# Value and output projection in chunks of 512 tokens in place of halves of a batch

## The chip, the cores and the metric

One core of a Trainium2 chip. The metric is device time in microseconds (us) of one execution. The engines are TensorE (PE: matrix products; PEld: its weight loads), VectorE (DVE), ScalarE (ACT), GpSimd (POOL) and SyncE (SP), which here only issues DMA transfers. The five run side by side, each through its own list in order.

## The reference

Sparse attention over 8 batches, 8 heads, 576 tokens and head size 64, then a gated projection of the 512 wide result:

```python
scores = scale * np.matmul(q, k.transpose(0, 1, 3, 2))
# heads 0-3: 0 <= i - j < 32; heads 4-7: j <= i and j % 32 == i % 32
attn = softmax(np.where(masks, scores, -1e9))
x = (attn @ v)                        # put together to [8, 576, 512]
gate_pre = sum(conv_w[k] * xp[:, k:k + S, :] for k in range(5))
gate = 1.0 / (1.0 + np.exp(-gate_pre))
val = x @ w_val                       # 512 x 512
return gate * val @ w_out             # 512 x 512
```

## The kernel before, in words

Features lie on the partitions (four blocks of 128, `ct` or `e`), tokens on the free axis. For each batch `b`:

- **Attention.** `attend_local` (three units) and `attend_strided` (two) make scores in PSUM (`s_ps`), a softmax on VectorE, ScalarE and GpSimd, a transpose of the weights (`t_ps` or VectorE), and the product with `v` (`x_ps`). ScalarE copies it into `xs[b % 2]`.
- **Splitting.** `split_x` writes x as a rounded part `xhi` (ScalarE) and a rest `xlo` (VectorE for `ct` 0 and 1, GpSimd for 2 and 3), so that three fast products `hi·hi`, `hi·lo`, `lo·hi` stand for one exact product. There is one pair of buffers for even and one for odd batches.
- **Gate.** `gate` runs the five-tap convolution along the tokens on VectorE, four instructions of 576 columns for each `e`, between two ScalarE instructions. For `e` 0 and 1 of batch 0, TensorE does it with diagonal matrices, which VectorE builds (128x640) in `ghi`. There is one gate buffer for each `e`.
- **Value.** `value` (line 450) takes each batch in two halves of 288 tokens: 8 groups (4 `e` x 2 halves) of 12 matmuls into one of three `m_ps` banks. VectorE multiplies the bank by the gate into `GV` (two buffers), ScalarE rounds it into `ghi`, and GpSimd writes the rest into `glo`.
- **Projection.** `project` (line 473) takes 128 tokens at a time: 12 matmuls of 512 columns over `ghi`, `glo` and `wo`, a ScalarE copy into `osb` and a DMA to `out`. 576 is 4.5 x 128, so an even batch leaves 64 tokens, which ScalarE copies to the front of `ghi` and `glo` for the next batch (`CARRY`).

Weights come as float64 and are made on the chip (`weight_rows`): each quarter is loaded, unpacked by ScalarE and VectorE, rounded by ScalarE, and its rest is written by GpSimd. For `w_val` the buffers `gate0` to `gate3` serve as scratch, for `w_out` two buffers `w64`.

All steps are recorded first and then issued in a written order, the string `SEQUENCE`. A token is a step's number; `f0x4` is four filler matmuls on zeros (line 162), which write a bank that nobody reads. Each engine, and SP with its DMA issues, keeps this order, and waits where an operand is not ready or a buffer is not free.

Of the kernel before, what the change touches and what calls it, by code (L numbers as in the profile page):

```python
# [18 lines left out]
DM = 512  # L19
# [7 lines left out]
CARRY = S % P  # L27
# [30 lines left out]
def tile_sparse_attention_moe(  # L58
# [68 lines left out]
    xhp = tiles(2, [P, 4, PADK + S], "xhi", F32R)  # L127
    xlp = tiles(2, [P, 4, PADK + S], "xlo", F32R)
    xhi, xlo = [t[:, :, PADK:] for t in xhp], [t[:, :, PADK:] for t in xlp]
    ghi = pool.tile([P, 4, CARRY + S], F32R, name="ghi")  # L130
    glo = pool.tile([P, 4, CARRY + S], F32R, name="glo")
    diags = ghi[:, :, :]
# [5 lines left out]
    gates = tiles(4, [P, S], "gate")  # L138
# [12 lines left out]
    w64 = tiles(2, [P, DM], "w64")  # L151
# [7 lines left out]
    idle = pool.tile([P, 512], BF16, name="idle")  # L159
    V.memset(idle, 0.0)  # L160
    plan.spare = [t[:, :] for t in m_ps.items[::-1] + x_ps.items]
    plan.filler = lambda at: T.matmul(out=at, lhsT=idle[:, :P], rhs=idle[:, :], start=True, stop=True)  # L162
# [138 lines left out]
    def attend_local(b):  # L301
# [3 lines left out]
        for u in range(3):  # L305
# [58 lines left out]
            if b in DIRECT:  # L364
                hi, lo = xhi[b % 2][:, 0:2, part], xlo[b % 2][:, 0:2, part]
# [55 lines left out]
    def gate(b):  # L421
        xs = xss[b % 2]
        for e in range(4):
            gt, group = gates[e], f"G{b}.{e}"
            if (b, e) in CONV:

                dg = diags[:, 2 * e:2 * e + 2, :].rearrange("p h (k w) -> p h k w", k=KC)
# [22 lines left out]
    def value(b):  # L450
        for e, hf in [(e, hf) for e in range(4) for hf in range(2)] if b in VORD else [(e, hf) for hf in range(2) for e in range(4)]:
            group = f"V{b}.{e}.{hf}"
            c0 = CARRY + hf * HALF
            x0 = hf * HALF
            vp = m_ps.next()[:, :HALF]
            terms = [(w, xx, ct) for ct in range(4)
                     for w, xx in ((wv[0], xhi[b % 2]), (wv[1], xhi[b % 2]), (wv[0], xlo[b % 2]))]
            pe(group, [
                mm(vp, w[:, ct, e * P:(e + 1) * P], xx[:, ct, x0:x0 + HALF], i == 0, i == 11)
                for i, (w, xx, ct) in enumerate(terms)])  # L460
            hi, lo = ghi[:, e, c0:c0 + HALF], glo[:, e, c0:c0 + HALF]
            held = (b, e, hf) in HELD

            gv = vp if held else GV.next()[:, :]
            dve(group, V.scalar_tensor_tensor, out=gv, in0=gates[e][:, x0:x0 + HALF], scalar=1.0, in1=vp,
                op0=ALU.add, op1=ALU.mult)
            act(group, A.copy, out=hi, in_=gv)
            if held:
                dve(group, V.tensor_tensor, out=lo, in0=gv, in1=hi.bitcast(F32), op=ALU.subtract)
            else:  # L470
                gps(group, G.tensor_tensor, out=lo, in0=gv, in1=hi.bitcast(F32), op=ALU.subtract)

    def project(b):

        odd = b % 2
        for m in range(4 + odd):
            group = f"P{b}.{m}"
            op = m_ps.next()[:, :]
            c0 = m * P + (0 if odd else CARRY)
            terms = [(gg, w, e) for e in range(4) for gg, w in ((ghi, wo[0]), (ghi, wo[1]), (glo, wo[0]))]  # L480
            pe(group, [
                mm(op, gg[:, e, c0:c0 + P], w[:, e, :], i == 0, i == 11)
                for i, (gg, w, e) in enumerate(terms)])
            osb = OSB.next()
            act(group, A.activation, out=osb, in_=op, func=AF.Copy, scale=0.5)
            r0 = b * S + m * P - (CARRY if odd else 0)
            plan.add("sp", group,
                     [(nc.sync.dma_start, dict(out=out[r0:r0 + P, :], in_=osb))])
# [8 lines left out]
    from_f64("make cw", cw64.rearrange("p c k w -> p (c k) w"), *[t[:, :4 * KC] for t in w64], whole=cw.rearrange("p c k -> p (c k)"))  # L497
# [24 lines left out]
NB = 1  # L522
PACKED = {4, 5, 6, 7}
VORD = {2, 3, 4, 5, 6, 7}
CONV = {(0, 0), (0, 1)}
ONPE = {(0, "L", u) for u in range(3)}
HELD = set()
DIRECT = {0}
SEQUENCE = """
72 18 0 23 44 30 38 68 1 3 5 17 73 32 22 2 74 71 70 37 75 7 4 21 50 8 9 19 175 40 11 46 6 76 10 25 81 12 20 15 78 27 45  # L530
13 39 14 79 24 41 16 f0x4 f0x1 f0x12 87 47 80 88 48 103 89 33 49 90 104 105 91 52 26 106 34 f0x6 119 92 107 42 93 176
120 108 269 95 121 29 94 272 205 36 96 51 77 122 99 43 109 123 53 98 f0x5 135 199 110 97 86 153 31 136 270 137 111 177
271 112 138 124 56 154 139 125 113 126 140 114 155 127 115 178 35 206 156 f0x4 100 200 128 101 273 141 116 102 130 142
62 129 143 117 85 284 54 118 83 131 299 144 55 179 84 132 157 82 57 158 201 58 181 147 285 276 159 160 278 63 64 275
207 286 145 65 133 287 146 134 148 59 161 288 151 300 60 180 149 162 66 314 289 152 61 301 202 165 445 183 166 277 163
290 292 444 164 291 182 447 171 302 150 184 172 67 f0x2 293 315 203 167 173 217 283 174 279 168 351 187 169 208 352 446
# [91 lines left out]
```

## Time and profile before

| | us |
|---|---|
| Runs: median of 3 (lowest, highest) | 309.85 (308.98, 310.96) |
| Profiled execution, its own time | 311.87 |
| Profiled execution, span | 309.9 |
| TensorE busy | 298.4 (96%) |
| VectorE busy | 231.7 (75%) |
| ScalarE busy | 228.8 (74%) |
| GpSimd busy | 192.7 (62%) |

The span runs from the first to the last instruction. A matmul's busy time overlaps its neighbours', since matmuls are pipelined: what one costs in a row of them is the distance between starts, not its duration. The granted clock of TensorE was 0.994 of full speed on average.

### The profile page before, as it was taken

Reading aid. Unit: us, or ns where it says so; the run is one execution under the profiler, and the core shown is the slowest. Engines: PE = TensorE matmul, PEld = TensorE weight load, DVE = VectorE, ACT = ScalarE, POOL = GpSimd, SP = SyncE. Lnnn points to the kernel's source line nnn. Section 1 sums busy time; section 2 is a strip of 40 time slices with the busy share of each in tenths; the row PEclk is TensorE's granted clock in tenths of the full one; section 3 lists DMA queues with packets and bytes.
Section 4 is the critical chain, followed back from the end, with each engine's and each line's share of the span. In section 5 each row is a group of like instructions: output and inputs, shape, how many; then the busy total and the mean of one; then the engine's idle time right before and its main releaser. Section 6 shows DMA issues by size and latency. Waiting matters only on the chain.

```text
span 309.9 us, 11212 instructions
## 1 busy us (share of the span) xinstructions
PE 298.4 (96%) x4773; PEld 261.6 (84%) x4773; DVE 231.7 (75%) x407; ACT 228.8 (74%) x501; POOL 192.7 (62%) x236
## 2 busy tenths in 40 slices
PE   8778999999999999999999999999999999999995
PEld 2448789988899889998899988998899789989983
DVE  4498779989989759867998788798955787595200
ACT  6367976998689887979999787967987848635221
POOL 8284999977876784738758696567456412562410
PEclk9799999999999999999999999999999999999999
DMA  7889678637485287344445245400134020011003
GB/s 227 298 238 278 234 254 228 220 90 218 139 241 189 72 264 249 108 131 140 142 144 193 76 158 188 141 29 2 70 88 143 36 105 34 3 68 70 0 34 135
DMA packets 20321, 43.99 MB, mean 142 GB/s; under 512 B 3056, under 2 KB 8944, under 8 KB 19696
## 3 DMA queue, kind: packets, MB, share of 16 engines
q1 hardware_dynamic: 20272, 43.28, 43.7%
q8 instruction: 37, 0.61, 0.8%
q14 instruction: 12, 0.10, 0.1%
HBM read 33.84 MB, written 9.44 MB: 140 GB/s over the span
## 4 chain that ended last, share of the span: by engine, by line
PE 89%; DMA 6%; DVE 1%; ACT 1%; issue 1%; POOL 0%; SPq 0%; POOLq 0%
PE m_ps L53 66%; PE x_ps L53 10%; PE s_ps L53 9%; PE t_ps L53 4%; DMA xs<-in_w_val_dram 2%; DMA KBL<-in_kL_dram 2%; DMA KBS<-in_kS_dram 1%; DVE KBL L173 1%; PE m_ps L162 1%; DVE ST L53 0%; ACT BDS L53 0%; POOL PB L53 0%; SPq L53 0%; ACT gate L53 0%; ACT osb L53 0%
## 5 line engine op out<-in xcount | busy, mean ns | idle before, releaser
L53 DVE SCALAR_TENSOR_TENSOR gate<-xs,cw,gate 128x576 f32<-128x576 f32 x120 | 110.9, 943 | 4.8 <-ACT gate L53 4.0
L53 PE MATMUL m_ps<-xhi,wv 128*128 128x288 f32 x512 | 103.7, 297 | 0.0
L53 POOL TENSOR_TENSOR glo<-GV,ghi 128x288 fp32r<-128x288 f32 x64 | 56.0, 881 | 55.6 <-ACT ghi L53 55.2
L53 PE MATMUL m_ps<-wo,ghi 128*128 128x512 f32 x288 | 90.1, 394 | 0.0
L53 PEld LDWEIGHTS m_ps<-xhi,wv 128*128 128x128 f32 x512 | 82.1, 188 | 0.8
L53 PE MATMUL m_ps<-xlo,wv 128*128 128x288 f32 x256 | 75.6, 295 | 0.0
L53 PEld LDWEIGHTS m_ps<-wo,ghi 128*128 128x128 f32 x288 | 53.0, 188 | 11.1 <-issue 0.2
L53 PE MATMUL m_ps<-wo,glo 128*128 128x512 f32 x144 | 56.2, 390 | 0.0
L53 DVE SCALAR_TENSOR_TENSOR GV<-gate,m_ps 128x288 f32<-128x288 f32 x64 | 28.3, 446 | 33.4 <-POOL glo L53 14.2
L53 PEld LDWEIGHTS m_ps<-xlo,wv 128*128 128x128 f32 x256 | 48.1, 188 | 0.0
L53 POOL TENSOR_TENSOR PB<-SML,ST 128x128 f32<-128x128 f32 (+1 forms) x48 | 33.7, 715 | 19.6 <-DVE ST L53 13.6
L53 ACT CAST ghi<-GV 128x288 fp32r<-128x288 f32 x64 | 27.4, 431 | 19.7 <-DVE GV L53 19.3
L53 ACT COPY BDL<-t_ps 64x256 f32<-64x256 f32 (+2 forms) x108 | 34.3, 318 | 6.4 <-PE t_ps L53 4.8
L53 ACT COPY xs<-x_ps 128x288 f32<-128x288 f32 (+1 forms) x53 | 32.0, 610 | 9.4 <-PE x_ps L53 9.2
L53 ACT ACTIVATE osb<-m_ps 128x512 f32<-128x512 f32 x36 | 21.5, 600 | 21.5 <-PE m_ps L53 18.0
L53 PEld LDWEIGHTS m_ps<-wo,glo 128*128 128x128 f32 x144 | 27.0, 188 | 5.8
L53 ACT COPY BDS<-PT 32x288 f32<-32x288 f32 x64 | 27.7, 432 | 2.2 <-PE x_ps L53 1.0
L53 POOL TENSOR_TENSOR xlo<-xs,xhi 128x576 fp32r<-128x576 f32 x16 | 26.4, 1657 | 3.9 <-ACT xhi L53 3.8
L53 POOL TENSOR_TENSOR PS<-SMS,ST 128x256 f32<-128x256 f32 (+1 forms) x32 | 20.8, 664 | 12.3 <-DVE ST L53 12.3
L53 POOL TENSOR_TENSOR SML<-SML,ST 128x384 f32<-128x384 f32 x21 | 23.6, 1129 | 6.5 <-DVE ST L53 6.5
L53 DVE TENSOR_REDUCE ST<-SML 128x6 f32<-128x390 f32 (+1 forms) x45 | 24.3, 544 | 2.4 <-ACT SML L53 2.3
L53 ACT ACTIVATE gate<-xs,cw 128x576 f32<-128x576 f32 x30 | 23.2, 776 | 2.0 <-DVE GV L53 1.8
(91 smaller groups left out, 408.6 us busy)
## 6 DMA issues: line engine op xcount, KB each, us to landing
out_dram<-osb SPq DMA_DIRECT2D x36, 256.0 KB, 2.1
vLs<-in_vL_dram SPq DMA_DIRECT2D x8, 640.0 KB, 5.2
qLs<-in_qL_dram SPq DMA_DIRECT2D x16, 288.0 KB, 5.4
KBL<-in_kL_dram SPq DMA_DIRECT2D x16, 288.0 KB, 4.4
KBS<-in_kS_dram SPq DMA_DIRECT2D x16, 288.0 KB, 5.2
qSs<-in_qS_dram SPq DMA_DIRECT2D x16, 288.0 KB, 4.4
vSs<-in_vS_dram SPq DMA_DIRECT2D x32, 128.0 KB, 5.4
raw<-in_w_val_dram SPq DMA_DIRECT2D x2, 512.0 KB
```

Source lines behind the costliest of these rows:

```text
L53: fn(**kw)
L162: plan.filler = lambda at: T.matmul(out=at, lhsT=idle[:, :P], rhs=idle[:, :], start=True, stop=True)
L173: [(lambda out: eng.memset(out, value), dict(out=ap))])
```

## The change

`value` and `project` no longer go by batch but by chunk of the 4608 tokens in a row: seven chunks of 512, one of 448 (the rest of batch 6), and the last batch as two of 288. A value group is thus 12 matmuls of 512 columns instead of 288: 40 groups (28 of 512, 4 of 448, 8 of 288) in place of 64. The projection keeps its 36 groups of 12. `xhi` and `xlo` become one ring of 1024 columns each; `split_x` cuts where the ring or a special chunk ends (46 pieces for 30). `ghi` and `glo` hold one chunk (640 columns); the carry copies go. Each `gate` buffer holds two batches, and the second half is scratch for `w_out`. A gate multiplication is cut where the gate buffer wraps (52 for 64). The last projection's fifth group holds 64 tokens of batch 7 and 64 of batch 6, stored by two DMAs. The diagonals lie in `ghi` and `glo`. Fillers read a 128 wide zero tile four times over; there are 52 instead of 34. `SEQUENCE` is another.

```diff
+CH = 512
+GW = 640
+LAST = (B - 1) * S
+CHUNKS = [(CH * c, CH, CH * (c % 2), 0) for c in range(7)]
+CHUNKS += [(7 * CH, LAST - 7 * CH, 2 * CH - (LAST - 7 * CH), GW - (LAST - 7 * CH))]
+CHUNKS += [(LAST + i, HALF, i, i) for i in (0, HALF)]
...
-    xhp = tiles(2, [P, 4, PADK + S], "xhi", F32R)
-    xlp = tiles(2, [P, 4, PADK + S], "xlo", F32R)
-    ghi = pool.tile([P, 4, CARRY + S], F32R, name="ghi")
+    xhp = pool.tile([P, 4, PADK + 2 * CH], F32R, name="xhi")
+    xlp = pool.tile([P, 4, PADK + 2 * CH], F32R, name="xlo")
+    ghi = pool.tile([P, 4, GW], F32R, name="ghi")
...
-    gates = tiles(4, [P, S], "gate")
+    gates = tiles(4, [P, 2 * S], "gate")
-    GV = Ring(tiles(2, [P, HALF], "GV"))
+    GV = Ring(tiles(2, [P, CH], "GV"))
...
+    def place(t, n):
+        if t < 7 * CH:
+            return t % (2 * CH), min(n, 2 * CH - t % (2 * CH), 7 * CH - t)
+        if t < LAST:
+            return CHUNKS[7][2] + t - 7 * CH, min(n, LAST - t)
+        return t - LAST, n
...
+        done = 0
+        while done < S:
+            at, n = place(b * S + done, S - done)
+            hi, lo, x = xhi[:, ct, at:at + n], xlo[:, ct, at:at + n], xs[:, ct, PADK + done:PADK + done + n]
+            act(group, A.copy, out=hi, in_=x)
+            eng(group, fn, out=lo, in0=x, in1=hi.bitcast(F32), op=ALU.subtract)
+            done += n
...
+    def value(*chunks):
+        for e in range(4):
+            for c in chunks:
+                t, n, x0, g0 = CHUNKS[c]
+                vp = m_ps.next()[:, :n]
...
+                pe(group, [
+                    mm(vp, w[:, ct, e * P:(e + 1) * P], xx[:, ct, x0:x0 + n], i == 0, i == 11)
+                    for i, (w, xx, ct) in enumerate(terms)])
+                hi, lo = ghi[:, e, g0:g0 + n], glo[:, e, g0:g0 + n]
+                gv = GV.next()[:, :n]
+                cut = min(n, 2 * S - t % (2 * S))
+                for i, w in ((0, cut), (cut, n - cut)):
+                    if w:
+                        at = (t + i) % (2 * S)
+                        dve(group, V.scalar_tensor_tensor, out=gv[:, i:i + w], in0=gates[e][:, at:at + w], scalar=1.0,
+                            in1=vp[:, i:i + w], op0=ALU.add, op1=ALU.mult)
+                act(group, A.copy, out=hi, in_=gv)
                 gps(group, G.tensor_tensor, out=lo, in0=gv, in1=hi.bitcast(F32), op=ALU.subtract)
...
-        if not odd:
-            for gg in (ghi, glo):
-                act(f"P{b}.carry", A.copy, out=gg[:, :, 0:CARRY], in_=gg[:, :, S:S + CARRY].bitcast(F32))
...
+        for c in ((b,) if b < 6 else (6, 7) if b == 6 else ()):
+            value(c)
+            project(c)
+    value(8, 9)
+    project(8)
...
-72 18 0 23 44 30 38 68 1 3 5 17 73 32 22 2 74 71 70 37 75 7 4 21 50 8 9 19 175 40 11 46 6 76 10 25 81 12 20 15 78 27 45
+44 20 1 22 72 31 38 29 0 3 79 7 17 9 33 5 74 34 4 78 23 73 10 39 40 75 11 41 36 42 46 45 50 32 81 30 80 6 77 43 205 8
```

**SP's list at the start**, from the first load for batch 1 (before: the twelfth row of the list) to the last quarter of `w_val` (`xs<-in_w_val`). `qLs`, `KBL`, `vLs` are q, k, v of the local heads, `vSs` v of the strided ones. Before:

```order
L53 DMA qLs<-in_qL_dram 64x1152
L53 DMA KBL<-in_kL_dram 64x2x576
L53 DMA vLs<-in_vL_dram 128x5x256
L53 DMA vSs<-in_vS_dram 8x1x2048
L53 DMA qLs<-in_qL_dram 64x1152
L53 DMA KBL<-in_kL_dram 64x2x576
L53 DMA xs_78<-in_w_val_dram 128x1024
L53 DMA vLs<-in_vL_dram 96x256
L53 DMA xs_78<-in_w_val_dram 128x1024
```

In the change, from the twelfth row too, where `vLs` and the third quarter of `w_val` still belong to the first loads:

```order
L58 DMA vLs<-in_vL_dram 128x5x256
L58 DMA xs_78<-in_w_val_dram 128x1024
L58 DMA KBL<-in_kL_dram 64x2x576
L58 DMA vLs<-in_vL_dram 96x256
L58 DMA qLs<-in_qL_dram 64x1152 x2
L58 DMA KBL<-in_kL_dram 64x2x576
L58 DMA vSs<-in_vS_dram 16x2048
L58 DMA vLs<-in_vL_dram 96x256
L58 DMA xs_78<-in_w_val_dram 128x1024
```

The second `KBL` of batch 1 now stands ahead of the first `vSs`, and the third quarter of `w_val` ahead of all of batch 1; the last quarter still stands right behind the 96-row `vLs`. Ahead of the first scores, batch 0's two `qSs` and the first quarter of `w_val` now stand before its second `KBL`.

**TensorE's list just ahead of the first value product** (`m_ps<-xhi,wv`). `m_ps<-xhi,ghi` and `xlo,ghi` are the convolution by diagonals, `x_ps<-BDS,vSs` the strided product with v, `s_ps<-KBS` strided scores, `idle` a filler. Before:

```order
L53 MATMUL m_ps_125<-xhi_79,ghi 128x288 x2
L53 MATMUL m_ps_125<-xlo_81,ghi 128x288
L53 MATMUL s_ps_120<-KBS,qSs 32x36 x32
L53 MATMUL m_ps_126<-xhi_79,wv_85 128x288
L53 MATMUL m_ps_126<-xhi_79,wv_86 128x288
L53 MATMUL m_ps_126<-xlo_81,wv_85 128x288
```

In the change:

```order
L58 MATMUL m_ps_122<-xlo,ghi 128x288
L58 MATMUL t_ps_118<-ident,PB_104 128x128 x4
L58 MATMUL x_ps_119<-BDS_97,vSs 32x72 x16
L58 MATMUL s_ps_117<-KBS,qSs 32x36 x32
L166 LDWEIGHTS idle
L166 MATMUL m_ps_123<-idle 128x512
L166 LDWEIGHTS idle
L166 MATMUL m_ps_123<-idle 128x512
L58 MATMUL m_ps_122<-xhi,wv_83 128x512
```

One group of batch 1's strided scores, which stood right ahead of the value product, now stands behind it; two fillers stand in its place.

**TensorE's list where a chunk's value ends and its projection begins** (`m_ps<-wo,ghi`). Before, at the last batch, nothing lies between; a first projection there reads only the first half's tokens:

```order
L53 MATMUL m_ps_127<-xhi_80,wv_86 128x288
L53 MATMUL m_ps_127<-xlo_82,wv_85 128x288
L53 MATMUL m_ps_126<-wo_87,ghi 128x512
L53 MATMUL m_ps_126<-wo_88,ghi 128x512
L53 MATMUL m_ps_126<-wo_87,glo 128x512
```

In the change, at the fifth chunk, where least lies between:

```order
L58 MATMUL m_ps_121<-xhi,wv_84 128x512
L58 MATMUL m_ps_121<-xlo,wv_83 128x512
L58 MATMUL x_ps_120<-BDL_96,vLs 32x96 x16
L58 MATMUL m_ps_122<-wo_85,ghi 128x512
L58 MATMUL m_ps_122<-wo_86,ghi 128x512
L58 MATMUL m_ps_122<-wo_85,glo 128x512
```

One group of local products with v (`x_ps<-BDL,vLs`) stands between the last value matmul and the first projection, which reads all four `e` of that chunk.

## Rows read from the trace of the kernel before

**Rows 1.** The page, part 1: busy time, share of span, instructions by engine.

```profile
PE 298.4 (96%) x4773; PEld 261.6 (84%) x4773; DVE 231.7 (75%) x407; ACT 228.8 (74%) x501; POOL 192.7 (62%) x236
```

**Rows 2.** Chain that ended last, in time: start us, us, what.

```profile
22.25 7.47 DMA xs<-in_w_val_dram
...
43.78 3.38 PE m_ps L53 x24
...
50.63 0.66 PE s_ps L53 x24
51.29 0.66 PE x_ps L53 x32
...
267.21 39.02 PE m_ps L53 x216
...
306.25 0.60 ACT osb L53
```

**Rows 3.** One stretch: us, busy us (instructions) of each engine, PEclk, DMA, GB/s.

```profile
43.78:267.21 223.43, 223.21 (x3821) 201.72 (x3821) 183.75 (x321) 182.70 (x407) 149.34 (x169) 1.00 0.44 137
```

**Rows 4.** TensorE in order, two steady stretches near the end: start us, us, what.

```profile
282.90 0.42 PE L53 MATMUL m_ps<-xhi,wv 128*128 128x288 f32 x2
...
292.02 0.42 PE L53 MATMUL m_ps<-xhi,wv 128*128 128x288 f32 x2
...
292.42 0.63 PE L53 MATMUL m_ps<-wo,ghi 128*128 128x512 f32 x2
...
303.33 0.61 PE L53 MATMUL m_ps<-wo,ghi 128*128 128x512 f32 x2
```

**Rows 5.** TensorE in order, the first 44 us; brackets: idle before, releaser.

```profile
9.72 1.50 PE L53 MATMUL s_ps<-KBL,qLs 128*32 128x128 f32 x24 [2.29 <-DMA KBL<-in_kL_dram]
...
25.50 1.52 PE L53 MATMUL s_ps<-KBL,qLs 128*32 128x128 f32 x48 [0.85 <-DVE ghi L53]
...
32.23 1.07 PE L53 MATMUL x_ps<-BDS,vSs 128*32 128x72 f32 x52 [0.35 <-ACT BDS L53]
33.65 0.38 PE L53 MATMUL x_ps<-BDS,vSs 128*32 128x72 f32 x10 [0.36 <-issue]
...
43.49 0.28 PE L53 MATMUL s_ps<-KBS,qSs 128*32 128x36 f32 x9 [0.53 <-issue]
43.71 0.53 PE L53 MATMUL m_ps<-xhi,wv 128*128 128x288 f32 x2
```

**Rows 6.** SyncE's DMA issues in order, the first 30 us.

```profile
16.65 0.58 SPq L53 DMA_DIRECT2D vLs<-in_vL_dram  x1
18.33 0.68 SPq L53 DMA_DIRECT2D vSs<-in_vS_dram  x1
...
19.60 0.59 SPq L53 DMA_DIRECT2D KBL<-in_kL_dram  x1
...
22.25 0.98 SPq L53 DMA_DIRECT2D xs<-in_w_val_dram  x1
```

**Rows 7.** Groups by shape: out<-in shapes xcount | busy, mean ns | idle before.

```profile
L53 POOL TENSOR_TENSOR glo<-GV,ghi 128x288 fp32r<-128x288 f32 x64 | 56.0, 881 | 55.6 <-ACT ghi L53 55.2 <-POOL glo L53 0.3
...
L53 DVE SCALAR_TENSOR_TENSOR GV<-gate,m_ps 128x288 f32<-128x288 f32 x64 | 28.3, 446 | 33.4 <-POOL glo L53 14.2 <-PE m_ps L53 14.0 <-ACT gate L53 3.9
...
L53 ACT CAST ghi<-GV 128x288 fp32r<-128x288 f32 x64 | 27.4, 431 | 19.7 <-DVE GV L53 19.3
...
L53 POOL TENSOR_TENSOR wv<-gate,wv 128x512 fp32r<-128x512 f32 x4 | 5.6, 1392 | 1.3 <-ACT wv L53 1.3
...
L53 DVE SCALAR_TENSOR_TENSOR gate<-gate,gate 128x512 uint32<-128x512 uint32 x4 | 2.9, 718 | 0.0
...
L53 ACT CAST wv<-gate 128x512 fp32r<-128x512 f32 x4 | 2.4, 618 | 0.4 <-DVE gate L53 0.4
```

**Rows 8.** Groups by shape: the longest single instructions of VectorE and GpSimd.

```profile
L53 DVE SCALAR_TENSOR_TENSOR gate<-xs,cw,gate 128x576 f32<-128x576 f32 x120 | 110.9, 943 | 4.8 <-ACT gate L53 4.0
...
L53 POOL TENSOR_TENSOR xlo<-xs,xhi 128x576 fp32r<-128x576 f32 x16 | 26.4, 1657 | 3.9 <-ACT xhi L53 3.8
```

More of the change, by code (lines that the diff above doesn't have):

```diff
@@ L126, in tile_sparse_attention_moe @@
     xss = tiles(2, [P, 4, PADK + S], "xs")
-    xhp = tiles(2, [P, 4, PADK + S], "xhi", F32R)
-    xlp = tiles(2, [P, 4, PADK + S], "xlo", F32R)
-    xhi, xlo = [t[:, :, PADK:] for t in xhp], [t[:, :, PADK:] for t in xlp]
-    ghi = pool.tile([P, 4, CARRY + S], F32R, name="ghi")
-    glo = pool.tile([P, 4, CARRY + S], F32R, name="glo")
-    diags = ghi[:, :, :]
+    xhp = pool.tile([P, 4, PADK + 2 * CH], F32R, name="xhi")
+    xlp = pool.tile([P, 4, PADK + 2 * CH], F32R, name="xlo")
+    xhi, xlo = xhp[:, :, PADK:], xlp[:, :, PADK:]
+    ghi = pool.tile([P, 4, GW], F32R, name="ghi")
+    glo = pool.tile([P, 4, GW], F32R, name="glo")
+    diags = [t.rearrange("p e c -> p (e c)")[:, :2 * KC * P] for t in (ghi, glo)]
     wv = tiles(2, [P, 4, DM], "wv", F32R)
@@ L156, in tile_sparse_attention_moe @@
     m_ps = Ring(tiles(3, [P, 512], "m_ps", space=psum))
-    idle = pool.tile([P, 512], BF16, name="idle")
+    idle = pool.tile([P, P], BF16, name="idle")
     V.memset(idle, 0.0)
     plan.spare = [t[:, :] for t in m_ps.items[::-1] + x_ps.items]
-    plan.filler = lambda at: T.matmul(out=at, lhsT=idle[:, :P], rhs=idle[:, :], start=True, stop=True)
+    plan.filler = lambda at: T.matmul(out=at.rearrange("p (n w) -> p n w", w=P), lhsT=idle[:, :],
+                                      rhs=idle[:, None, :].to_broadcast([P, 4, P]), start=True, stop=True)
     none = pool.tile([P, 1], F32, name="none")
@@ L364, in attend_local @@
             if b in DIRECT:
-                hi, lo = xhi[b % 2][:, 0:2, part], xlo[b % 2][:, 0:2, part]
+                hi, lo = xhi[:, 0:2, part], xlo[:, 0:2, part]
                 act(group, A.copy, out=hi, in_=xp)
@@ L423, in gate @@
         for e in range(4):
-            gt, group = gates[e], f"G{b}.{e}"
+            gt, group = gates[e][:, b % 2 * S:b % 2 * S + S], f"G{b}.{e}"
             if (b, e) in CONV:
-                dg = diags[:, 2 * e:2 * e + 2, :].rearrange("p h (k w) -> p h k w", k=KC)
+                dg = diags[e].rearrange("p (h k w) -> p h k w", h=2, k=KC)
                 wide = [P, KC, P]
@@ L448, in gate @@
             act(group, A.activation, out=gt[:, :], in_=gt[:, :], func=AF.Tanh, scale=0.5)
[L450 to L470, printed above, removed]
-                gps(group, G.tensor_tensor, out=lo, in0=gv, in1=hi.bitcast(F32), op=ALU.subtract)
@@ L473, in project @@
[L473 to L477, printed above, removed]
+    def value(*chunks):
+        for e in range(4):
+            for c in chunks:
+                t, n, x0, g0 = CHUNKS[c]
+                group = f"V{c}.{e}"
+                vp = m_ps.next()[:, :n]
+                terms = [(w, xx, ct) for ct in range(4) for w, xx in ((wv[0], xhi), (wv[1], xhi), (wv[0], xlo))]
+                pe(group, [
[10 more added lines that the diff above has]
+                act(group, A.copy, out=hi, in_=gv)
+                gps(group, G.tensor_tensor, out=lo, in0=gv, in1=hi.bitcast(F32), op=ALU.subtract)
@@ L478, in project @@
+    def project(c):
+        t, n, _, g0 = CHUNKS[c]
+        if c == 8:
+            n = GW
+        for m in range(n // P):
+            group = f"P{c}.{m}"
             op = m_ps.next()[:, :]
-            c0 = m * P + (0 if odd else CARRY)
             terms = [(gg, w, e) for e in range(4) for gg, w in ((ghi, wo[0]), (ghi, wo[1]), (glo, wo[0]))]
+            c0 = g0 + m * P
             pe(group, [
@@ L485, in project @@
             act(group, A.activation, out=osb, in_=op, func=AF.Copy, scale=0.5)
-            r0 = b * S + m * P - (CARRY if odd else 0)
-            plan.add("sp", group,
-                     [(nc.sync.dma_start, dict(out=out[r0:r0 + P, :], in_=osb))])
-        if not odd:
-            for gg in (ghi, glo):
-                act(f"P{b}.carry", A.copy, out=gg[:, :, 0:CARRY], in_=gg[:, :, S:S + CARRY].bitcast(F32))
+            r0 = t + m * P
+            parts = [(r0, 0, P)]
+            if r0 + P > B * S:
+                own = B * S - r0
+                parts = [(r0, 0, own), (LAST - (P - own), own, P)]
+            for r, p0, p1 in parts:
+                plan.add("sp", group,
+                         [(nc.sync.dma_start, dict(out=out[r:r + p1 - p0, :], in_=osb[p0:p1, :]))])
     flat = xss[1].rearrange("p c s -> p (c s)")
@@ L514, in tile_sparse_attention_moe @@
             for e in range(4):
-                weight_rows(f"wo{e}", w_out, wo, e, raws[(4, 0, 1, 4)[e]], *[t[:, :] for t in w64])
+                weight_rows(f"wo{e}", w_out, wo, e, raws[(4, 0, 1, 4)[e]],
+                            *[t[:, S:S + DM] for t in (gates[e % 2], gates[2 + e % 2])])
         gate(b)
-        value(b)
-        project(b)
+        for c in ((b,) if b < 6 else (6, 7) if b == 6 else ()):
[3 more added lines that the diff above has]
+    project(8)
     plan.issue(SEQUENCE)
@@ L522 @@
 NB = 1
+DIRECT = {0}
 PACKED = {4, 5, 6, 7}
[L524 removed]
 CONV = {(0, 0), (0, 1)}
 ONPE = {(0, "L", u) for u in range(3)}
[L527 to L528 removed]
 SEQUENCE = """
[L530 to L532 removed]
```

22 lines of the change are left out of this document (10 added, 12 removed), and 94 rows, old and new, of the table SEQUENCE.

## The prediction

> **What bounds the kernel now.** I read the busy shares first, then the chain that ended last, then single stretches. TensorE is busy 96% of the span, VectorE, ScalarE and GpSimd 75, 74 and 62% [rows 1]. Busy time overstates a pipelined engine, so the chain decides: near 43.7 us, where the value products begin, it comes to TensorE and stays there but for a few small pieces, up to the last 39.02 us of 216 matmuls and a ScalarE copy at 306.25 [rows 2]; the stretch table shows TensorE busy 223.21 of 223.43 us up to those 39 [rows 3]. Ahead of 43.7 the chain goes through other things, among them the last quarter of `w_val`, 7.47 us under way [rows 2]. So the end is the start of the first value product, plus TensorE's work behind it, plus the time TensorE is kept waiting there, plus a tail of 3.7 us (the span of 309.9 less 267.21 + 39.02).
>
> **The change part by part.**
>
> *The value matmuls.* What one costs is the distance between starts. In the last value run 69 matmuls of 288 columns start within 292.02 - 282.90 = 9.12 us, 0.1322 each; in the last projection 48 of 512 columns within 303.33 - 292.42 = 10.91, 0.2273 each [rows 4]. 224 more columns cost 0.0951 us, so 64 fewer than 512 leave 0.2273 - 0.0272 = 0.2001 for 448. Before there are 64 x 12 = 768 of 288: 101.5 us. In the change 336 of 512 (76.4), 48 of 448 (9.6) and 96 of 288 (12.7): 98.7. That is **-2.9** (unrounded), the fixed share of 288 instructions, some 0.01 us each. No row shows a value matmul of 512 columns, which moves `xhi` and not `wo`. If its time went with the columns alone (0.1322 x 512/288 = 0.2350), nothing would be gained; the projection's row, the same width and type, is nearer, and I take it. The Trainium skill ("TensorE: Matmul & The Clock Gate", Back-to-back issue gap) gives a warm gap of N/2.4 + 2.5 ns; by it the 288 instructions would be worth 0.7 us. The rows lie above that rule at both widths (132.2 ns against 122.5, 227.3 against 215.8), so I go by them.
>
> *The start.* By the order shown, TensorE's list between batch 1's first local scores and the first value product keeps its work, but for one group of strided scores moved behind it. Before, this stretch took 43.71 - 25.50 = 18.2 us, with idle pieces of 0.35, 0.36 and 0.53 [rows 5]. Less one group of scores, at up to 0.66 [rows 2], it is 17.6; without the idle pieces 16.3. Where does it begin? Its scores need the second `KBL` of batch 1, issued at 19.60. Ahead of that SP stood from 17.23 (16.65 + 0.58) to 18.33 and then issued `vSs` for 0.68 [rows 6]; in the change `vSs` stands behind, so the load goes up to 1.8 us earlier and the stretch begins between 23.7 and 25.5. The first value product then starts between 40.0 and 43.1. Against the early end speak two things. Batch 0's first scores, which waited 2.29 us for `KBL` [rows 5], now stand behind two more loads (`qSs`); at worst that wait comes a second time and moves all by 2.3, to 45.4. And the last quarter of `w_val` waits behind a `vLs` load as before, with its unpacking ahead of work that TensorE needs. I take 41.2, nearer to the early end, since the third quarter no longer stands behind batch 1's loads: **-2.5**. The 18 more fillers stand in these waits; where a wait is shorter than its fillers, they cost what they take, 0.2 us each by the 512-column rows. The moved group of scores lies behind the value start now: **+0.6**.
>
> *The handoff from value to projection.* Behind a value group come VectorE's product, ScalarE's rounding and GpSimd's rest: 0.446 + 0.431 + 0.881 = 1.76 us at 288 columns. At 512 the nearest rows of that width have 0.718, 0.618 and 1.392: 2.73 [rows 7]. The first projection behind a chunk needs the last `e` rounded at its tenth matmul (2.05 us in) and the rest at its twelfth (11 x 0.2273 = 2.50 in), so 0.23 us of other TensorE work in between is enough. At the fifth chunk, the tightest of the 512 ones, one group of local products stands there, 0.66 [rows 2]. That covers it if the three engines are free at once; VectorE may be in a gate instruction (0.943) and GpSimd in a rest of x (1.657) [rows 8]. Bounds: -1, since wider groups hold a PSUM bank longer and two batches of gates let VectorE run ahead (TensorE's small losses between groups, put at a microsecond), to +5.9 (below). I take **+0.5**, near the stretch of before, where 0.22 us was idle.
>
> *The rings.* The split of a batch now waits until the chunk before is read; before, a batch two back. Between a chunk's last and the next one's first value matmul lie four projection groups (48 x 0.2273 = 10.9 us) and attention. Copy, rounding and two rests on GpSimd need some 5 (2 x 1.657 and two ScalarE instructions of 0.6 to 0.7). I cost it at nothing; without that cover TensorE would wait ahead of value groups as the second rival has it ahead of projections.
>
> *Beside it.* VectorE: 12 gate products fewer, no wait for a free gate, 8 pieces of `xlo` more. ScalarE: 24 roundings of the gated value and 8 carry copies fewer, 16 of x more. GpSimd: 24 rests of the gated value fewer, 8 of x more. All lie beside TensorE's work, on engines with a quarter of their time free. SP's extra store is not the last of its list and lies beside a projection of 2.7 us: nothing.
>
> **Sum:** -2.9 - 2.5 + 0.6 + 0.5 = -4.3 us. The profiled execution's 311.87 us becomes 307.6, its span 305.6. It stands 2.0 above the median of the runs, 309.85, so for that I forecast **305.5 us**. Ends: a start at 40.0, the full -2.9 and -1 give 302.8; a start at 45.4, nothing by width and +5.9 give 318.
>
> **Rivals.** 1% of the median, 3.1 us, is about what a measurement of this kernel can tell from no change.
>
> - *The start gains nothing* (0.18). The last quarter of `w_val` lands as late as before, and fillers take what was won. For it: it stands behind the same `vLs`, in a full queue. Against: `KBL` of batch 1 no longer waits for `vSs`. First value product at 43.7: 305.5 + 2.5 = 308.0.
> - *The handoff is exposed* (0.17), the one that ends slower. Each chain comes behind one long instruction on two engines, 0.943 + 1.657 = 2.6 us late. The work between value and projection, in groups of some 0.6, is 2.2 us at the fourth chunk, 0.7 at the fifth, 1.3 at the seventh and 1.2 at the eighth, each less the 0.23; the others have 3 and more. Lost: 0.6 + 2.1 + 1.5 + 1.7 = 5.9. 305.5 - 0.5 + 5.9 = 310.9. It turns the result once 4.9 us are lost there. For it: GpSimd's rests take 1.4 us now, in a list in fixed order. Against: the chain alone fits everywhere.
> - *The width gains nothing* (0.10): cost by columns alone, 305.5 + 2.9 = 308.4. For it: no row has this operand at 512. Against: the projection's row. By the skill's rule above it would be 307.7.
> - *As forecast* (0.55).
>
> **How the numbers follow.** The forecast's own case, 302.8 to 307.5, is faster by over 1% (under 306.75) in some nine parts of ten: 0.50; the start rival adds 0.03 and the width rival 0.02. Slower by over 1% (over 312.95) is four parts in ten of the handoff rival, 0.07, and 0.03 for two mishaps at once. The rest, 0.35, is within 1%. The range 302.8 to 310.0 holds the forecast's case and nearly all of the start and width rivals; it leaves out most of the handoff rival.
>
> **What the profile after would show.** Starts of value matmuls 0.227 us apart (right) or 0.235 (wrong). The first of them at 41 us, or, if the start rival holds, at 43 and later, with idle TensorE before it that ends on `KBL` or `w_val`. Behind it TensorE without idle time; where the handoff rival holds, waits on `glo` or `ghi` ahead of projections; where the ring does, on `xlo` or `xhi` ahead of value groups. The forecast is wrong if TensorE's idle time behind the first value product passes 3 us, or the first value product comes after 43.

## The result, and the profile after

The change took **312.76 us** (median of 6 runs, 311.79 to 315.34), the kernel before beside it 309.37 (308.56 to 310.96): **ratio 1.0117, 95% interval 1.0073 to 1.0162**, slower by 1.2%. The forecast was 305.5. Run once more on another chip the change was 1.0127 (1.0090 to 1.0164), so this holds. The profiled execution took 311.79 us, its span 310.0. Of 95 further executions of the kernel before, 88 have a mean granted clock of at least 0.997 and a median of 309.9 us, seven at most 0.995 and 312.2 us; the profile before (0.994, 311.87 us) is like the seven, that of the change (0.998) like the 88.

The busy times of the page answer to [rows 1]:

```profile
PE 301.8 (97%) x4503; PEld 243.2 (78%) x4503; DVE 233.8 (75%) x403; ACT 223.9 (72%) x485; POOL 182.1 (59%) x220
```

TensorE has 270 matmul records fewer and is busy 3.4 us longer; GpSimd and ScalarE got the relief that the change promised them, and it was worth nothing, since neither of them set TensorE's pace. The chain of waits (start us, us, what) answers to [rows 2]:

```profile
39.90 5.74 PE m_ps L58 x24
...
271.58 34.77 PE m_ps L58 x192
306.35 0.02 issue
306.38 0.60 ACT osb L58
```

It still comes to TensorE at the first value product and ends in one long stretch and a copy. The stretch between (us, busy us of PE, PEld, DVE, ACT, POOL, then granted clock, DMA share, GB/s), against [rows 3]:

```profile
39.55:306.38 266.83, 265.37 (x3814) 218.12 (x3812) 203.95 (x344) 195.30 (x425) 153.38 (x167) 1.00 0.38 122
```

TensorE is idle for only 1.5 us in 266.8: by idle time nothing is wrong. Yet from the start of the first value product to that of the last matmul the change needs 266.4 us, where the trace before had 262.1 (43.71 [rows 5] to 305.83). The first value product and the last matmul of the change, then the last matmul before:

```profile
39.55 0.82 PE L58 MATMUL m_ps<-xhi,wv 128*128 128x512 f32 x2
...
305.95 0.39 PE L58 MATMUL m_ps<-wo,glo 128*128 128x512 f32 x1
...
305.83 0.39 PE L53 MATMUL m_ps<-wo,glo 128*128 128x512 f32 x1
```

So the loss must be read from start to start of the matmuls. TensorE in order in a run of 36 value matmuls (start us, us, form, number), against [rows 4]:

```profile
73.75 0.63 PE L58 MATMUL m_ps<-xhi,wv 128*128 128x512 f32 x2
...
80.76 0.63 PE L58 MATMUL m_ps<-xhi,wv 128*128 128x512 f32 x2
```

Thirty matmuls in 7.01 us, 0.2337 each; over the undisturbed steps of the trace, some 290, the mean is 0.2326, where 0.2273 was forecast. The same view where the sixth chunk's value products begin (in brackets idle time before, and what ended it):

```profile
202.12 0.62 PE L58 MATMUL m_ps<-xhi,wv 128*128 128x512 f32 x2
202.58 0.40 PE L58 MATMUL m_ps<-xlo,wv 128*128 128x512 f32 x1
203.33 0.73 PE L58 MATMUL m_ps<-xhi,wv 128*128 128x512 f32 x2 [0.35 <-ACT xhi L58]
204.54 0.50 PE L58 MATMUL m_ps<-xlo,wv 128*128 128x512 f32 x1 [0.47 <-POOL xlo L58]
204.88 0.63 PE L58 MATMUL m_ps<-xhi,wv 128*128 128x512 f32 x2
```

From 202.12 to 204.88 two groups of three matmuls took 2.76 us, not 1.40: TensorE waits 1.4 us for the copy and the rest of x, though the brackets admit only 0.82. ScalarE in order just before shows why the copy was late:

```profile
202.44 0.60 ACT L58 ACTIVATE osb<-m_ps 128x512 f32<-128x512 f32 x1 [1.99 <-DMA out_dram<-osb]
202.94 0.34 ACT L58 CAST xhi<-xs 128x192 fp32r<-128x192 f32 x1
203.31 0.26 ACT L58 COPY BDL<-t_ps 32x128 f32<-32x128 f32 x1
203.57 0.51 ACT L58 CAST xhi<-xs 128x384 fp32r<-128x384 f32 x1
```

It stood 1.99 us for an output buffer's store, with the copy of x queued behind. The handoff costs were sized well; the groups by shape (mean ns behind the comma), against [rows 7]:

```profile
L58 POOL TENSOR_TENSOR glo<-GV,ghi 128x512 fp32r<-128x512 f32 x28 | 38.5, 1381 | 19.8 <-ACT ghi L58 19.0 <-POOL glo L58 0.6
L58 ACT CAST ghi<-GV 128x512 fp32r<-128x512 f32 x28 | 17.1, 618 | 6.1 <-DVE GV L58 5.8
...
L58 DVE SCALAR_TENSOR_TENSOR GV<-gate,m_ps 128x512 f32<-128x512 f32 x16 | 10.7, 671 | 4.9 <-ACT gate L58 4.2 <-PE m_ps L58 0.7
```

### The profile page after: what moved, and what is told of

The parts are those of the page before. It is cut to its first block, busy times and chain, and to the rows that moved or that the text cites. A ratio compares the mean times of both kernels' runs of the same rounds, so it can differ in the third digit from the quotient of the medians.

```text
span 310.0 us, 10604 instructions
## 1 busy us (share of the span) xinstructions
PE 301.8 (97%) x4503; PEld 243.2 (78%) x4503; DVE 233.8 (75%) x403; ACT 223.9 (72%) x485; POOL 182.1 (59%) x220
## 4 chain that ended last, share of the span: by engine, by line
PE 83%; DVE 5%; DMA 5%; SPq 2%; ACT 1%; POOL 1%; issue 1%; POOLq 0%; DVEq 0%
PE m_ps L58 62%; PE x_ps L58 10%; PE s_ps L58 7%; PE t_ps L58 3%; DVE gate L58 3%; SPq L58 2%; DMA osb<-in_w_out_dram 2%; DMA KBL<-in_kL_dram 2%; PE m_ps L166 1%; DMA out_dram<-osb 1%; DVE ST L58 1%; DVE KBL L178 1%; ACT gate L58 1%; POOL SML L58 0%; POOL xlo L58 0%
## 5 line engine op out<-in xcount | busy, mean ns | idle before, releaser
L58 PE MATMUL m_ps<-xhi,wv 128*128 128x512 f32 (+2 forms) x320 | 93.9, 377 | 0.4 <-ACT xhi L58 0.4
L58 POOL TENSOR_TENSOR glo<-GV,ghi 128x512 fp32r<-128x512 f32 (+2 forms) x40 | 50.3, 1265 | 35.9 <-ACT ghi L58 34.4
L58 PEld LDWEIGHTS m_ps<-xhi,wv 128*128 128x128 f32 x320 | 57.1, 188 | 11.0 <-ACT xhi L58 0.8
L58 PE MATMUL m_ps<-xlo,wv 128*128 128x512 f32 (+2 forms) x160 | 59.6, 373 | 0.5 <-POOL xlo L58 0.5
L58 POOL TENSOR_TENSOR PB<-SML,ST 128x256 f32<-128x256 f32 (+1 forms) x48 | 32.0, 681 | 25.1 <-DVE ST L58 13.8
L58 DVE SCALAR_TENSOR_TENSOR GV<-gate,m_ps 128x512 f32<-128x512 f32 (+5 forms) x52 | 25.9, 511 | 21.4 <-PE m_ps L58 11.4
L58 POOL TENSOR_TENSOR xlo<-xs,xhi 128x576 fp32r<-128x576 f32 (+6 forms) x24 | 29.9, 1251 | 17.6 <-ACT xhi L58 17.6
L58 PEld LDWEIGHTS m_ps<-xlo,wv 128*128 128x128 f32 x160 | 30.0, 188 | 6.4 <-POOL xlo L58 1.2
L58 ACT CAST ghi<-GV 128x512 fp32r<-128x512 f32 (+2 forms) x40 | 22.7, 576 | 14.9 <-DVE GV L58 14.6
L58 ACT CAST xhi<-xs 128x576 fp32r<-128x576 f32 (+6 forms) x46 | 23.1, 504 | 0.3
```

Of the source, the lines that this page charges most:

```text
L58: fn(**kw)
```

## The experiments

Ratios are to the kernel before on the same chip, with 95% intervals. A "step" is the time from one matmul's start to the next one's, averaged over the undisturbed ones of a trace.

**1. The kernel before, again** (no edit).

> The kernel before once more, for a second trace of it. Its profiled execution took 311.87 us, 2.5 above the median of its runs, while that of the change, 311.79, is the shortest of its six. Theory 'odd run': the first trace of the kernel before holds some 2 us of waits that its other executions do not have, so what it showed from the first value product on (262.1 us) is 2 us too long and the change is worse there than the two traces say; a second trace takes 309 to 310 and shows where. Rival 'start': the 2 us lie ahead of the first value product, in loads, and what stands behind it stays at 262 us.

310.04 us, ratio 0.9999 (0.9964 to 1.0034). TensorE in order at the first value product and at the last matmul:

```profile
40.62 0.53 PE L53 MATMUL m_ps<-xhi,wv 128*128 128x288 f32 x2
...
48.20 0.54 PE L53 MATMUL x_ps<-BDL,vLs 128*32 128x96 f32 x16 [1.01 <-DMA vLs<-in_vL_dram]
...
304.01 0.39 PE L53 MATMUL m_ps<-wo,glo 128*128 128x512 f32 x1
```

The rival held: the first value product starts at 40.62, not at 43.71 as in [rows 5], since the last quarter of `w_val` was issued at 20.22, not 22.25 [rows 2]. Behind it stand 263.4 us in place of 262.1: part of an early start is lost at once, to a `vLs` load. The 2.0 us by which the profiled execution stood above the median lay in this start.

They come from the first 15 us. In the first trace TensorE waited 2.29 us for batch 0's `KBL` before its first scores at 9.72 [rows 5]; here it waits less:

```profile
9.11 0.86 PE L53 MATMUL s_ps<-KBL,qLs 128*32 128x128 f32 x24 [1.29 <-DMA KBL<-in_kL_dram]
```

In the first trace the same 24 matmuls take 1.50 us, and the next 24 take 1.48. Its granted clock was 0.51 from 9.50 to 13.00 us, near the lower level of 1.2 GHz, here 1.00. Its page shows the fall in the second of 40 slices:

```profile
PEclk9799999999999999999999999999999999999999
```

The third group of 24 started at 14.57 there and at 12.53 here, and these 2.0 us stay up to the load of `w_val`. So the profile that the prediction started from had lost 2 us to a longer wait and a lower clock; by the clocks of the 95 executions above, most lose nothing there.

**2. The change, again** (no edit).

> The change once more, beside the kernel before on the same chip, for a second trace. The two traces of the kernel before differ by 3.1 us in the start of the first value product (43.7 and 40.6 us) and only by 1.3 behind it (262.1 and 263.4). Theory 'scatter at the start': the change too starts its value products within some 2 us of 39.9, and keeps 266 us behind them with the wait on x at 203 us in the same place; the ratio is again some 1.010. Rival: the 266 us were an odd run, and a second trace shows 264 or less, the ratio nearer to 1.003.

314.05 us, ratio 1.0127 (1.0090 to 1.0164). First value product at 41.53, last matmul at 308.40: 266.9 us behind it, against 266.4. The wait at 205 us came again, smaller (0.7 us); another grew, which had been 0.3:

```profile
237.02 0.39 PE L58 MATMUL m_ps<-xlo,wv 128*128 128x512 f32 x1
238.25 0.73 PE L58 MATMUL m_ps<-xhi,wv 128*128 128x512 f32 x2 [0.84 <-ACT osb L58]
```

Here the second value group of the seventh chunk wants an accumulation bank that ScalarE has not emptied, because it waits for a store (2.33 us in ScalarE's row at 237.60). Together both places cost 1.7 us in either trace.

**3. Six output buffers in place of two.**

```diff
-    OSB = Ring([osb2[:, i, :] for i in range(2)])
+    OSB = Ring([osb2[:, i, :] for i in range(2)] + [t[:, DM * i:DM * i + DM] for t in raw for i in range(2)])
```

> The change with six output buffers in place of two (four of them the halves of `raw`, which is done after the start). In the trace ScalarE waits 7.9 us for the stores of `osb`, one of these waits (2.0 us at 202.4) in front of the copies of x for the sixth chunk, whose value group then waits some 1.4 us on `xhi` and `xlo`. Theory 'ring': these waits set the copies late; the wait at 203 us goes or shrinks and the time falls by 1 to 1.5 us, to some 311.5. Rival 'gates': the rests of x stand behind gate instructions on VectorE and work on GpSimd anyway, and the waits stay; 312.8.

311.86 us, ratio 1.0063 (1.0037 to 1.0089), and 265.4 us behind the first value product: 1.0 to 1.5 less. The bank wait is gone; at 204 us TensorE still loses 0.6 to the rest of x, behind GpSimd's work on the local scores. Both theories were half right.

**4. Rows of x on whole multiples of 64 bytes**, in the change (shown) and in the kernel before (there with 592 columns a row).

```diff
-    xhp = pool.tile([P, 4, PADK + 2 * CH], F32R, name="xhi")
-    xlp = pool.tile([P, 4, PADK + 2 * CH], F32R, name="xlo")
-    xhi, xlo = xhp[:, :, PADK:], xlp[:, :, PADK:]
+    flats = [pool.tile([P, 16 + 8 * CH], F32R, name=n) for n in ("xhi", "xlo")]
+    xhi, xlo = [t[:, 16:].rearrange("p (c s) -> p c s", c=4) for t in flats]
...
```

> The change with the rows of `xhi` and `xlo` 4096 bytes apart (before the edit 4112) and their data 64 bytes behind the tile's start (before 16), as the rows of `wo` are a multiple of 64 bytes apart with the data at the tile's start. Theory 'placement': a 512-column value matmul takes 0.233 us and not the 0.227 of a projection because of where its moving operand lies; value steps fall to 0.227, 336 x 0.006 = 2.0 us less, some 310.7 us. Rival 'operand': x costs more because three engines write it while TensorE reads it, or because the weights change at every matmul; steps stay at 0.233 and the time at 312.8.

> The kernel before with the rows of `xhi` and `xlo` 2368 bytes apart (before the edit 2320) and their data 64 bytes behind the tile's start (before 16). Placement: if 288 columns lose as much to it as 512 do (0.006 us a matmul), value steps fall from 0.132 to 0.126 and 768 x 0.006 = 4.6 us go, some 304.8 us; then the width's prediction failed since both widths pay the same and the projection does not. Operand: steps stay at 0.132, the time at 309.4.

312.71 us, ratio 1.0077 (1.0042 to 1.0113), step 0.2336; the kernel before so edited 310.65, 1.0027 (1.0001 to 1.0054), step 0.1327. There is no gain, so placement in this sense fell.

**5. Equal weights side by side.**

```diff
-                terms = [(w, xx, ct) for ct in range(4) for w, xx in ((wv[0], xhi), (wv[1], xhi), (wv[0], xlo))]
+                terms = [(w, xx, ct) for ct in range(4) for w, xx in ((wv[1], xhi), (wv[0], xhi), (wv[0], xlo))]
```

> The change with the three products of a value group in the order `wv1`*`xhi`, `wv0`*`xhi`, `wv0`*`xlo`, so that the same weights stand in two neighbouring matmuls, as `ghi` does in a projection; in the change they alternate. Theory 'weights': the 512-column value step is 0.2326 us and the projection's 0.227 because of the alternating weights; steps fall to 0.227 and the time by 336 x 0.0055 = 1.8 us. Rival 'moving operand': steps stay at 0.232 to 0.233, time as the change's.

313.09 us, ratio 1.0103 (1.0055 to 1.0152), step 0.2324: it is not the weights.

**6. Value matmuls that move `wo`**, first in chunks 1 to 6 (shown), then in the last three (`c >= 7`). Their products are of other data: the value of x is left out, and only the times mean something.

```diff
+                if 1 <= c <= 6:
+                    terms = [(w, wo[0] if xx is xhi else wo[1], ct) for w, xx, ct in terms]
+                    x0 = 0
```

> The change, with the value matmuls of chunks 1 to 6 moving `wo` in place of x (the value products are left out in that sense: they multiply other data). So no value group of those chunks waits for a copy or rest of x, and the moving operand is the projection's. Theory 'ring': TensorE's waits on `xhi` and `xlo` at 203 us (1.4 us) and 236 us (0.2 us) go, and nothing of the length takes their place: 1.5 us less. Theory 'moving operand': steps of 512 columns fall from 0.2326 to 0.227, 288 x 0.0055 = 1.6 us less; together some 3 us below the change. Rival 'weights': the steps stay at 0.2326, and only the 1.5 us of waits go. Rival 'gates': the waits only move, to the gate products or the m_ps banks, and the time stays at the change's.

> The change with the value matmuls of the last three chunks (448, 288 and 288 columns) moving `wo` in place of x; their products are of other data. It shows the step of `wo` at two more widths, where x takes 0.204 us (448) and 0.1323 (288). Theory 'two operands': x and `wo` lie on different lines, and the prediction's line, drawn from x at 288 to `wo` at 512, was between them; with `wo` the steps fall below x's, by some 0.003 to 0.005 us, as they did at 512 (0.2326 to 0.227). Rival 'width': only wide x matmuls are dear, at 288 columns the two are alike (0.132), and the line of the prediction would have held for `wo`: 0.200 at 448.

The first: 311.57 us, ratio 1.0050 (1.0019 to 1.0080), 264.8 us behind the first value product. The run shown above at 73.75, now one row, as its records touch:

```profile
73.58 8.45 PE L58 MATMUL m_ps<-wo,wv 128*128 128x512 f32 x36
```

These are 36 matmuls in 8.45 us. The mean step of such matmuls is 0.2280, as in this trace's projections (0.2282), where x took 0.2326. So the step hangs on which operand moves. Without waits on x and with the shorter step 1.6 to 2.1 us go, where some 3 were expected: the 512-column value matmuls took 2.7 us less, and the rest came back elsewhere, 0.4 of it in a wait on `glo` at 60 us.

The second was executed once (313.63 us): 0.2027 at 448 columns and 0.1316 at 288, where x took 0.2040 and 0.1323. There the rival is nearer: at 288 the operands are nearly alike, and `wo`'s own steps at 288 and 448 point to 0.231 at 512. The 0.2280 measured there lies below that, so it belongs to no line through the narrower widths.

**7. x behind `wo` in the on-chip memory**, in the change (shown) and in the kernel before.

```diff
-    xhp = pool.tile([P, 4, PADK + 2 * CH], F32R, name="xhi")
-    xlp = pool.tile([P, 4, PADK + 2 * CH], F32R, name="xlo")
...
     wo = tiles(2, [P, 4, DM], "wo", F32R)
+    xhp = pool.tile([P, 4, PADK + 2 * CH], F32R, name="xhi")
+    xlp = pool.tile([P, 4, PADK + 2 * CH], F32R, name="xlo")
...
```

> The change with `xhi` and `xlo` placed behind `wo` in the on-chip memory, and the gated value and the weights 33 kB further down; nothing else differs. With `wo` as the moving operand the 512-column value step fell from 0.2326 us to 0.227, while rows on whole multiples of 64 bytes left it at 0.2336. Theory 'place': the operand's place in the memory sets the step; the value steps fall to 0.227 (1.9 us less), and the projection, whose `wo` now lies lower, may rise to 0.233. Rival 'operand itself': it is what is in x or what else uses it, wherever it lies; steps stay at 0.2326 and 0.227 and the time as the change's.

> The kernel before with the same new placement. Place: the 288-column steps fall from 0.132 by as much a column as the 512-column ones of the change, 0.003 us each, 768 x 0.003 = 2.4 us less, less what the projections lose. Operand itself: no difference.

312.80 us, ratio 1.0096 (1.0066 to 1.0126), and 310.05, 1.0004 (0.9982 to 1.0026). The 512-column step fell to 0.2306, not quite half of the way to a projection's mean of 0.2283; projections and 288-column steps (0.1321) stayed. At 448 columns it fell from 0.2040 to 0.2026, which is what `wo` took there. By the steps this is worth 0.7 us, but the trace shows no gain: 267.6 us stand behind the first value product, 0.7 to 1.2 more than in the change, with longer waits on x, on `glo` and on an accumulation bank.

**8. The width alone**: each 512-column group as two of 256.

```diff
+                cuts = (0, 256) if n == CH else (0,)
+                wide = n // len(cuts)
...
-                    for i, (w, xx, ct) in enumerate(terms)])
...
+                    for h in cuts for i, (w, xx, ct) in enumerate(terms)])
```

> The change with each 512-column value group computed as two groups of 256 columns, one after the other, in the same place of the order (672 matmuls in place of 336). It prices the width alone. By the line that the prediction drew (0.1322 us at 288 columns, 0.4246 ns a column) a 256-column step would take 0.1186, and two 0.2372; if the fixed share is that large, the change loses 336 x (0.2372 - 0.2326) = 1.5 us by it, and 3.3 if 512 columns could be had in 0.2273. By the columns alone, from 0.2326 at 512, a step takes 0.1163 and nothing changes. From the value rows alone (0.1322 at 288, 0.2326 at 512) it is 0.1179, and 1.1 us are lost.

321.40 us, ratio 1.0357 (1.0308 to 1.0405). The median step is 0.118, two make 0.236: with 0.1323 at 288, 0.2040 at 448 and 0.2326 at 512, x's steps lie on one straight line of 0.448 ns a column and a fixed share of 3 ns, not the 10 ns that the prediction drew. That is some 1.2 us for 336 pairs. The rest of the 8.6 us more than the change took is no price of width: behind the first value product TensorE waits 7.8 us by the profile, on x and elsewhere, where the change has 1.3. Why so many waits opened was not tested. The longest:

```profile
209.59 0.28 PE L58 MATMUL m_ps<-xlo,wv 128*128 128x256 f32 x1
211.96 0.62 PE L58 MATMUL m_ps<-xhi,wv 128*128 128x256 f32 x2 [2.09 <-ACT xhi L58]
```

TensorE stood 2.1 us there, and then one of the stretches of 3 us shows the granted clock (behind the busy times) at 0.53, near the lower level of 1.2 GHz:

```profile
209.00:212.00 3.00, 0.91 (x9) 0.71 (x7) 1.49 (x2) 0.90 (x3) 0.16 (x2) 1.00 0.84 267
212.00:215.00 3.00, 2.94 (x13) 2.64 (x14) 1.42 (x3) 2.89 (x8) 3.00 (x6) 0.53 0.52 188
215.00:218.00 3.00, 3.00 (x25) 3.00 (x25) 1.12 (x3) 1.69 (x5) 0.89 (x1) 0.90 0.23 87
```

**9. Fewer entries into wide runs.** An entry is a place where TensorE goes from attention's small matmuls to a run of value or projection matmuls. Only numbers of the order move: `245` directly behind `239`, `899` behind `896`, `395` behind `399`, `719` behind `715`, `1065` behind `1061`.

> The change with five groups of value or projection matmuls issued earlier, each directly behind the group before it (the third projection of chunk 0, the second of chunk 4, a value group of chunks 1, 3 and 5), so that TensorE enters such runs 29 times in place of 34; the kernel before has 28. Theory 'switches': in the traces of both kernels the first 512-column step of a run takes 0.314 to 0.34 us and the last one 0.318, against 0.227, some 0.18 us a run; five runs fewer give 0.9 us back, some 0.3% less than the change. Rival 'cover': the attention groups that now come later were waited for by VectorE and ScalarE, and the waits that follow take the 0.9 us or more; no gain, or up to 2 us slower.

326.94 us, ratio 1.0545 (1.0489 to 1.0601): the rival held, and its price of up to 2 us was far too low, as the kernel is 14 us slower than the change. What TensorE waited for in the whole span (total us, times, longest):

```profile
PE x_ps L58 <- ACT BDL L58: 5.0, 3, 2.5
PE x_ps L58 <- ACT BDS L58: 4.0, 2, 2.7
...
PE s_ps L58 <- DVE SML L58: 1.4, 2, 1.2
```

Behind the first value product all its waits add up to 11.2 us in this view, in the change to 1.3. An attention group that now comes later delays the copies on ScalarE and VectorE that the next group waits for. After the 2.72 us wait that ended at 71.39 the clock fell here too:

```profile
72.00:76.00 4.00, 4.00 (x48) 3.23 (x37) 3.48 (x6) 3.94 (x7) 2.33 (x3) 0.58 0.58 182
```

So this run could not price the entries.

**10. More entries, where no wait can open**: four small matmuls in each of the last 12 gaps.

```diff
+            if token == "r":
+                for fn, kw in self.steps[1388][2][:4]:
+                    fn(**kw)
+                continue
```

> The change with four small matmuls (a repeat of the last attention products, 32 x 72 each; their result is not used) put into each of the 12 gaps between the last 13 value and projection groups, where nothing else is left for TensorE. In the traces of before and change the four take some 0.07 us. Theory 'switches': each time TensorE goes from wide to small matmuls and back it loses some 0.09 us on either side beside the matmuls' own time, so the last stretch grows by 12 x (0.18 + 0.07) = 3.0 us; then the change's six more entries (34 in place of 28) cost 1.1 us. Rival 'no price': the dear first and last steps stand in the records but overlap with the small matmuls; the stretch grows by 12 x 0.07 = 0.8 us.

317.85 us, ratio 1.0243 (1.0208 to 1.0277). TensorE in order around one gap:

```profile
283.04 0.29 PE L62 MATMUL m_ps<-xlo,wv 128*128 128x288 f32 x1
283.27 0.33 PE L57 MATMUL x_ps<-BDS,vSs 128*32 128x72 f32 x8
283.53 0.53 PE L62 MATMUL m_ps<-xhi,wv 128*128 128x288 f32 x2
283.89 0.29 PE L62 MATMUL m_ps<-xlo,wv 128*128 128x288 f32 x1
```

From the first 288-column matmul to the last start the stretch grew from 26.15 us (279.80 to 305.95) to 31.78 (281.58 to 313.36): 0.47 a gap. The four matmuls are eight in the records, 0.14 us by the mean of such steps, so a round trip costs **0.33 us**, more than expected: 0.09 on the last wide step (0.225 in place of 0.1323), 0.10 on the first wide one (0.235), and, not foreseen, some 0.13 on the small ones, most of it on the last (0.156).

**11. Three mends at once**: six output buffers, x behind `wo`, and the late copy and rest of x one place earlier (numbers `1025` behind `1019`, `1026` behind `1020`).

> The change with three things at once: six output buffers in place of two, `xhi` and `xlo` placed behind `wo`, and the copy and rest of x of the last tile's 192 columns in chunk 5 issued one place earlier on ScalarE and GpSimd (ahead of a copy to an output buffer and of work on the strided scores). It sums up the account: the output buffers took 1.1 us out of the waits behind the first value product, the earlier copy should take most of the 0.5 us that TensorE still waited there at 204 us, and the placement takes 336 x 0.002 = 0.7 us. Behind the first value product then some 264.3 us stand in place of 266.6, and the time is 0.7% below the change's: ratio 1.003 to 1.006 to the kernel before, not faster than it, since the runs entered more often (1.1 us) and the strided group moved behind (0.9 us) stay. If the account is wrong, the waits come back elsewhere and the ratio stays near that of the six buffers alone, 1.006, or the change's, 1.012.

310.69 us, ratio 1.0040 (1.0018 to 1.0062), and 264.5 us behind the first value product, where 264.3 were expected. The account of these three terms holds; it says nothing on the price of the entries, which stay. No version here beats the kernel before.

## Why the prediction was wrong

The forecast had 1.8 us less behind the first value product (-2.9 + 0.6 + 0.5). Two traces of either kernel give 262.1 and 263.4 before, 266.4 and 266.9 after: 3.9 more. By its steps:

- **Value matmuls, -2.9: the step that failed first.** It took the projection's 0.2273 for 512 columns of x because that row was "the same width and type" (the 0.2273 is one stretch; over all projections of the trace the mean is 0.228). Measured: 336 x 0.2326 + 48 x 0.2040 + 96 x 0.1323 = 100.6 us, against 101.5: **-0.9**. The rival by columns alone, 0.2350, was nearer. Runs 6 and 8 show that x has its own line and that `wo` at 512 falls off even its own. The rule of the Trainium skill ("TensorE: Matmul & The Clock Gate", Back-to-back issue gap), N/2.4 + 2.5 ns for a warm matmul by itself, agrees with no step here (204.0 at 448 columns, 232.6 at 512, against 189.2 and 215.8), but its small fixed share was nearer to x's 3 ns than the 10 ns drawn.
- **Entries into wide runs, nothing: they are not in the sum.** The order as written has 34 from the first value product on, before 28. At up to 0.33 us each (run 10) six more are up to +2.0. Summed step by step, what the first and last wide steps and the last small ones took beyond the mean of their kind is 3.9 us in the trace before and 6.2 in the change: **+2.3**. It is more than six times 0.33, since fewer of the small groups ahead of an entry end in transposes (17 of 33, before 18 of 27), whose last step stays at 0.03. The wider groups were cut up more often by attention. It could have been counted before the run from the order and from the first and last steps of a run.
- **The rings, nothing: wrong by +1.7.** The copies of x need some 5 us in a cover of 10.9, as argued, but the sum left out what is queued ahead of them on ScalarE: copies into output buffers that wait for stores. Run 3 took 1.0 to 1.5 of it away, run 11 the rest.
- **Handoff, +0.5:** measured next to nothing in the first trace and 0.4 in the second, a wait on `glo` ahead of a projection (59.9 us and 62.4 us), 0.2 in the mean. The sizes were right, and the rival that it is exposed fell.
- **The moved group, +0.6:** 0.7 by 64 more records at 0.0104.
- **The start, -2.5 to 41.2:** the first value product came at 39.55 and 41.53, around the place forecast, but this was in part luck. The 43.71 that it was counted from belongs to the one trace of four with the lower clock at the start (run 1); the other three have 40.62, 41.10 and 41.75 (runs 1, 7 and 4). Twelve traces with the start of the change lie at 39.5 to 41.5. By the means of these three and twelve, 41.2 and 40.2, the gain is some 1.0. It was taken off a median of runs that mostly had the earlier start. Nor did it come as argued: the second `KBL` of batch 1 goes out at 17.54 in the change and went out at 17.56 in the second trace of before, so a `vSs` load less ahead of it did not bring it forward. The two lines of the change:

```profile
17.54 0.60 SPq L58 DMA_DIRECT2D KBL<-in_kL_dram  x1
...
22.59 0.86 PE L58 MATMUL s_ps<-KBL,qLs 128*32 128x128 f32 x24
```

From this group on, the first of batch 1, the change takes 17.0 us to the first value product; the second trace of before takes 17.4, from 23.22.

-0.9 + 2.3 + 1.7 + 0.2 + 0.7 = 4.0, where 3.9 us were measured. So close a match is luck: two traces of the kernel before differ by 1.3 us in this stretch, 1.0 of it the `vLs` wait of run 1, and small waits inside attention (0.2 to 0.4 us) have no term. With -1.0 at the start some 2.9 us remain of the 3.9, inside the interval of the measured ratio (2.3 to 5.0 us).

Of the tests named, the step's (0.227 or 0.235) told right. The limit of 3 us of idle time told nothing: 1.5 us idle, and 5.7 lost against the forecast, since long steps and round trips count as busy. What stays open is why `wo` at 512 columns is quicker than x: 64-byte rows and the order of weights are excluded, the place in memory gave 0.002 of the 0.0043 between the means (0.2326 and 0.2283). Nor is it that other engines write x meanwhile, a rival of run 4: in the trace of the change 38 steps during a write to x take 0.2324, 249 without one 0.2325.

## What to carry to other kernels

Price a matmul by steps of the operand that it will move; where no row has it at the new width, a line through its own widths is safer than another operand's row. Count how often a new order sends TensorE from wide to small matmuls and back, and look through the queue ahead of each copy that a shared buffer makes urgent. Before a stretch of one profile is subtracted from a median of runs, see from a second trace whether that stretch scatters, and from the granted clock whether the profiled execution was like most others: 0.994 on the page was the sign here.

## What the runs showed of the hardware

- A round trip from 128-wide to 32-wide matmuls and back cost 0.33 us, of which the last wide step took 0.09, the first wide one 0.10 and the small ones 0.13 (run 10).
- A wait of TensorE of 2.1 us was followed by a stretch at a granted clock of 0.53 (run 8), one of 2.7 us by one at 0.58 (run 9). A wait of 2.0 us in run 8 (at 159.6 us) left it at 1.00, as did the waits of 0.5 to 0.8 us in the change, so these traces give no length of a wait that decides.
- With the granted clock at 0.51, 24 matmuls of 128 columns took 1.50 us in place of 0.86 (first trace of the kernel before, and run 1).
- Moving the tiles of x 53 kB up in the memory shortened the 512-column step from 0.2326 to 0.2306 us (run 7).
